# Attention with a pooled branch and a wave MLP: q and k loaded as nine tokens a partition, turned whole and pooled on VectorE

## The chip, the core and the metric

The kernel runs on one core of a Trainium2 chip. A core has a matrix engine (TensorE, PE in the profile, with its weight loads as PEld), a vector engine (DVE), a scalar engine (ACT), a general engine (GpSimd, POOL) and a queue that issues DMAs (SyncE, SP). Operands lie in SBUF, memory of 128 partitions; matrix results go to PSUM, eight banks of 2 KB a partition. The metric is the device time in microseconds of one execution, as the median over runs.

## The reference, cut to what matters

```python
batch, n_heads, seq, head_dim = (8, 8, 576, 64)
# attention, per batch and head
q_d, k_d, v_d = (t.reshape(B, H, 144, 4, D).mean(axis=3) for t in (q, k, v))
out_up = np.repeat(softmax(scale * q_d @ k_d.T) @ v_d, 4, axis=2)
mask = np.abs(pos[:, None] - pos[None, :]) < 4
out_local = softmax(np.where(mask, scale * q @ k.T, -1e9)) @ v
x = (out_up + out_local) as [B, 576, 512]
# wave MLP
theta = x @ w_theta
y = w_tok_r @ (x * cos(theta)) + w_tok_i @ (x * sin(theta))     # over the tokens
u = x + y
out = u + np.maximum(u @ w_ch, 0.0)
```

All inputs and the output are float32; the kernel computes in bfloat16 with float32 sums.

## The kernel before

The eight batches run one after another through the same steps, and the steps of several batches overlap. A string of 682 letters, `ORDER` (lines 85 to 93), says in which order the steps are issued; each letter takes the next step of its kind, through the batches in turn. `pin` (line 691) ties every instruction to the one before it on its engine, so that each engine, and SP's queue too, works through its instructions in the order of the string.

The letters: **L** loads a piece of q, k or v into a staging tile (`load`, line 102; `stage`, line 98; eight tiles of 1024 floats a partition, line 69). **C** casts it to bfloat16 (`cast`, line 131; on GpSimd, but q of batch 0 on ScalarE). **A** turns q and k so that the head's 64 columns lie on the partitions, and makes the pooled q and k; the last A of a batch pools v (`turns`, line 294). **S** makes scores and their exponentials (`scores`, line 376): the first two steps of a batch are the pooled ones, the other five are key chunks of at most 128 keys around a chunk of queries, of which GpSimd blanks all but the band (batch 0 has the band added on TensorE). **N** is the pooled branch's output (three steps), **V** the local one (five), **T** turns and adds the two (five), **H** makes theta, its cosine and sine (five), **Z** the modulated x (four), **X** mixes the tokens (five: four of nine matmuls of 512 columns and a short one), **R** is the channel matmul and **O** the last addition and the store (five each). **z** and **u** are transposing DMAs, **l**, **c** and **W** load, cast and turn the weights, **K** makes constants, **D** keeps TensorE warm.

In batches 0 and 1 (`WIDE`, line 35) q and k are loaded for two heads at once, twelve successive tokens to a partition, 96 partitions: runs of 3072 bytes. In the other batches a token is a partition, 96 to a chunk, and each run is the 64 floats of one head, 256 bytes. v is loaded by key chunks, in runs of 256 bytes, in every batch.

A turn of a token chunk (`turn`, line 325) is four matmuls whose moving operand `ip` is the identity of 96 beside a pooling matrix of 24 columns, so that one pass over 120 columns gives both the turned chunk and its pooled columns; ScalarE evacuates the turned part (line 332), VectorE the pooled q (line 334), ScalarE the pooled k, in up to two pieces (lines 336 to 341), into `kdP`, which has groups of 30 of 32 columns. A wide turn (`wide_turn`, line 303) is eight matmuls with the identity, the last four added up in PSUM for the pooled columns. There are twelve such steps a batch.

PSUM is cut into two tiles of two banks (`w2`, line 78), used in rotation by S, N and V, and four of one bank (`w1`, line 81), used by the others, the turns among them. The key chunks begin at 0, 116, 236, 356 and 448 (`KS`, line 30), each 128 wide.

The weights go through the same staging tiles: theta in two loads, the two token matrices in five each, the channel matrix in two (`weight_loads`, line 235); GpSimd casts them all (line 250).

Of the kernel before, what the change touches and what calls it, by code (L numbers as in the profile page):

```python
# [27 lines left out]
QS = [0, 120, 240, 360, 480]  # L28
QC = [120, 120, 120, 120, 96]
KS = [0, 116, 236, 356, 448]  # L30
KW = [128, 128, 128, 128, 128]
QN = [128, 128, 128, 128, 96]
NCH = 5

WIDE = 2
WR = 12
WP = S // WR
TR = 96
TP = TR // 4
TW = TR + TP  # L40
NG = 3
# [11 lines left out]
def kernel(  # L53
# [15 lines left out]
    stg = ctx.enter_context(tc.tile_pool(name="stg", bufs=8))  # L69
# [11 lines left out]
    def w1(name, dt=FP32):  # L81
# [4 lines left out]
        "LLLKKCCLLLDLLCKACAACALLLCKKCCKKACLLLAKACACALLAALLCASSCCCDDlSSAVAVCSACCAANNAASllcllcNSllLLcTTAlAVVAcC"  # L86
        "HVccllllDAcATTZLLAcccLLccHHSTDWWZCCWLCLSWSWWWWACLZLCSHlVWNNHzLCAALCCCLLSNZAATVAAAATASSXVAAXlCCCSCAVL"
        "LLLLXSVASCccCCTTSTCAASHNXHZVAHHANAuXAHLAACCSSLzLLCZZCCLLuLCRNROROOAVAVAARLLTZSSOXTTSSXVLAAACCCCVXAAT"
        "SSRTHHOVVXANAAAuXCAANAHZHVLLHzLLLLANSSRRRCOuOLOZCRCOZSSZLCTXLLLLACCCSSTTXAAHVVXAARCOATACCCVAANHTZHNA"
        "ZHVZHSzXNVAAXATSSCLLLCCLTZCASHXVZSXAAAVSAAXuAAALCCSSLLTTROLLLTHCCCVRNOHHNHCAXuzNAVAROASSZZLLuXROASVZ"  # L90
        "TTLLRCSSCCCXSOXVTAXAATSSRAAOHNVCLLLuACZCCXNAAXVANAVuROTHVHTRRROOuOVAAVHTHRSSOZRROzOTSROASSROZZHHNNXS"
        "SZTTXHVXHVNHXZXzZZVTXVTTuuXRVHHOTROROZTRRHHOOHXZXXZZzRuuXXOXXRRuOOROXRuRROORROROOO"
# [5 lines left out]
    def stage(b, key):  # L98
        t = staged[b, key] = stg.tile([P, 1024], FP32, tag="st", name=f"st{b}_{key}")
        return t  # L100

    def load(b):

        if b < WIDE:
            for hh in range(4):
                for nm, src in zip("qk", (q, k)):
                    nc.sync.dma_start(
                        out=stage(b, f"{nm}{hh}")[0:TR, 0:WR * D],
                        in_=src[b, 2 * hh:2 * hh + 2].rearrange("h (p r) d -> (h p) (r d)", r=WR),
                    )  # L110
                    yield
        else:
            for nm, src in zip("qk", (q, k)):
                for i in range(3):
                    t = stage(b, f"{nm}{i}")[0:TR].rearrange("p (c h d) -> p c h d", c=2, d=D)
                    for j in range(2):
                        c = 2 * i + j
                        nc.sync.dma_start(
                            out=t[:, j], in_=src[b, :, TR * c:TR * c + TR, :].rearrange("h p d -> p h d"),
                        )  # L120
                    yield
        for i in range(3):
            t = stage(b, f"v{i}").rearrange("p (c h d) -> p c h d", c=2, d=D)
            for c in range(2 * i, min(2 * i + 2, NCH)):
                nc.sync.dma_start(
                    out=t[0:KW[c], c % 2],
                    in_=v[b, :, KS[c]:KS[c] + KW[c], :].rearrange("h p d -> p h d"),
                )
            yield

    def cast(b):

        dims = [TR, 2, WR, 2, D] if b < WIDE else [TR, 6, H, D]
        q_tm = work.tile(dims, BF16, tag="q_tm", bufs=1, name=f"q_tm{b}")
        k_tm = work.tile(dims, BF16, tag="k_tm", bufs=1, name=f"k_tm{b}")
        v_w = v_ws[b % 2]
        inputs[b] = (q_tm, k_tm, v_w)
        eng = CASTS.get(b, CASTS[None])
        if b < WIDE:
            for hh in range(4):  # L140
                for i, dst in enumerate((q_tm, k_tm)):
                    eng[i](out=dst[:, hh // 2, :, hh % 2, :],
                           in_=staged.pop((b, f"{'qk'[i]}{hh}"))[0:TR, 0:WR * D].rearrange("p (r d) -> p r d", d=D))
                    yield
        else:
            for i, dst in enumerate((q_tm, k_tm)):
                for c in range(3):
                    eng[i](out=dst[0:TR, 2 * c:2 * c + 2].rearrange("p c h d -> p (c h d)"),  # L148
                           in_=staged.pop((b, f"{'qk'[i]}{c}"))[0:TR])
                    yield  # L150
        for i in range(3):
            t = staged.pop((b, f"v{i}")).rearrange("p (c h d) -> p c h d", c=2, d=D)
            n, rows = (2, P) if i < 2 else (1, KW[4])
            eng[2](out=v_w[0:rows, 2 * i:2 * i + n, :, 0:D], in_=t[0:rows, 0:n])  # L154
            yield
# [16 lines left out]

    ip = ones("ip", TW, 0.25)
    PU = [ones(f"pu{lo}", KP, 0.25) for lo in (0, 4, 32)]
    own = ones("own", 4, 1.0)
    bands = [ones(f"band{i}", P, 0.0) for i in range(3)]

    def constants():

        pool = ip[0:TR, TR:TW]  # L180
        select(pool, 0, [[-4, TP]], 1)
        select(pool, 3, [[4, TP]], -1)
        nc.vector.tensor_copy(out=ip[0:TR, 0:TR], in_=ident[0:TR, 0:TR])
        yield
# [12 lines left out]


    pihc = const.tile([P, 1], FP32, name="pihc")
    nc.vector.memset(pihc, PIH)  # L200


    kdPs = []
# [542 lines left out]
```

## Time and profile before

| what | value |
|---|---|
| median of 3 runs | 265.8 us (265.38 to 266.84) |
| profiled execution, its own time | 264.21 us |
| its span, from first to last instruction | 262.4 us |
| DMA, mean over the span | 190 GB/s, 49.81 MB, 132483 packets, of which 122592 under 512 bytes |
| mean granted TensorE clock | 0.97 |

The page of the profile gives the busy time of each engine, groups of like instructions with the line that issues them, and a chain of waits: followed back from the last instruction, at each step to what released it. In a group, the first number behind the bar is the busy time of all its instructions in us, the second the mean duration of one in ns, and behind the second bar stands how long the engine had been idle just before them, and who ended that. A busy PE is not PE at its peak, since matmuls overlap one another; the pace of a matmul is read from the chain, which gives start, length, line and count.

### The profile page before, as it was taken

How to read it: one execution, taken by the hardware profiler on the slowest of the kernel's cores; microseconds unless marked ns; L12 is line 12 of the kernel's file. 1: busy time of each engine (PE TensorE's matmuls, PEld its weight loads, DVE VectorE, ACT ScalarE, POOL GpSimd, SP SyncE). 2: the span in 40 equal slices, each digit the busy share in tenths (PEclk: the TensorE clock that was granted, in tenths of full speed). 3: DMA queues.
4: the chain of work that ended last, by engine and by line, in shares of the span. 5: the costliest groups of instructions: out<-in, count | busy, mean ns of one | idle time of the engine just before them, and what ended most of it. 6: DMA issues, size and time to landing. Idle time of an engine off the chain costs nothing.

```text
span 262.4 us, 7363 instructions
## 1 busy us (share of the span) xinstructions
PE 240.0 (91%) x2902; PEld 150.8 (57%) x2938; DVE 171.0 (65%) x391; ACT 169.1 (64%) x338; POOL 162.9 (62%) x196
## 2 busy tenths in 40 slices
PE   3689989969999999999999999999999999999990
PEld 1554755645557655855666566656755556555450
DVE  3331786773666867686885767857978658754552
ACT  3654587895599858986899978849569870340000
POOL 4556946989799879877597599794953750000000
PEclk9858999997999999999999999999999999999998
DMA  7999999999999999999997999999987108145186
GB/s 196 241 236 245 338 228 232 197 228 189 244 194 206 196 169 268 180 216 197 268 203 154 211 180 240 155 222 206 233 222 211 28 0 108 46 141 110 42 216 196
DMA packets 132483, 49.81 MB, mean 190 GB/s; under 512 B 122592, under 2 KB 124640, under 8 KB 132448
## 3 DMA queue, kind: packets, MB, share of 16 engines
q1 hardware_dynamic: 132448, 49.33, 92.8%
q8 instruction: 23, 0.38, 0.6%
q14 instruction: 12, 0.10, 0.1%
HBM read 34.11 MB, written 9.44 MB: 166 GB/s over the span
## 4 chain that ended last, share of the span: by engine, by line
PE 72%; DMA 12%; ACT 6%; POOL 4%; DVE 2%; issue 2%; SPq 1%; DVEq 0%; POOLq 0%; ACTq 0%
PE psu L616 22%; PE psr L646 9%; PE psth L559 8%; PE pstr L329 5%; DMA st_q<-in_q_dram 5%; PE psS L431 4%; PE psloc L503 3%; PE xTps L539 3%; DMA st_k<-in_k_dram 3%; PE psxt L598 3%; DMA out_dram<-osb 3%; PE psut L622 2%; DMA stw_tok<-in_moe_w_tok_i_dram 2%; PE wu L284 2%; PE pstr L308 2%
## 5 line engine op out<-in xcount | busy, mean ns | idle before, releaser
L616 PE MATMUL psu<-WT,z 128*128 128x512 bf16 x276 | 66.6, 381 | 0.9 <-issue 0.4
L439 ACT ACTIVATE pm<-psS 128x1024 bf16<-128x1024 f32 (+1 forms) x40 | 38.1, 991 | 8.5 <-PE psS L431 8.4
L616 PEld LDWEIGHTS <-z 128*128 128x128 bf16 x288 | 26.7, 98 | 29.1 <-issue 0.8
L446 POOL TENSOR_SCALAR_AFFINE_SELECT pm<-pm 128x1024 bf16<-128x1024 bf16 (+1 forms) x35 | 36.8, 1052 | 10.1 <-ACT pm L439 10.1
L617 DVE TENSOR_TENSOR uT<-psu,xT 128x512 bf16<-128x512 f32 x32 | 22.1, 690 | 28.6 <-PE psu L616 28.6
L448 POOL TENSOR_SCALAR_AFFINE_SELECT pm<-pm 128x1024 bf16<-128x1024 bf16 (+1 forms) x35 | 36.8, 1053 | 2.4
L564 ACT ACTIVATE cs<-psth,pihc 128x512 bf16<-128x512 f32 x32 | 22.0, 689 | 16.4 <-PE psth L559 10.5
L559 PE MATMUL psth<-wth,xT 128*128 128x512 bf16 x115 | 31.1, 380 | 0.7
L646 PE MATMUL psr<-wch,uT 128*128 128x512 bf16 x118 | 30.4, 380 | 0.5
L512 DVE TENSOR_TENSOR tmp<-psloc,rl 120x512 bf16<-120x512 f32 (+1 forms) x40 | 27.6, 691 | 1.4
L542 DVE TENSOR_TENSOR xT<-xTps,xdT 128x480 bf16<-128x480 bf16 (+2 forms) x48 | 24.9, 549 | 3.7 <-PE xTps L539 3.3
L668 DVE SCALAR_TENSOR_TENSOR osb<-psr,ur 128x512 f32<-128x512 f32 x32 | 21.6, 685 | 6.4 <-DMA out_dram<-osb 3.8
L154 POOL CAST v_w<-st_v 128x1024 bf16<-128x1024 f32 (+1 forms) x24 | 21.1, 896 | 6.2 <-DMA st_v<-in_v_dram 5.2
L148 POOL CAST k_tm<-st_k 96x1024 bf16<-96x1024 f32 x18 | 18.5, 1035 | 9.3 <-DMA st_k<-in_k_dram 9.3
L332 ACT CAST kT<-pstr 128x384 bf16<-128x384 f32 x36 | 17.8, 497 | 8.2 <-PE pstr L329 8.1
L148 POOL CAST q_tm<-st_q 96x1024 bf16<-96x1024 f32 x18 | 18.6, 1034 | 6.7 <-DMA st_q<-in_q_dram 5.4
L599 DVE TENSOR_TENSOR z<-psxt,cs 128x1024 bf16<-128x1024 bf16 x32 | 21.3, 681 | 1.7 <-PE psxt L598 1.2
L332 ACT CAST qT<-pstr 128x384 bf16<-128x384 f32 x36 | 16.0, 490 | 8.2 <-PE pstr L329 8.1
L565 ACT ACTIVATE cs<-psth 128x512 bf16<-128x512 f32 x32 | 19.0, 594 | 0.0
L503 PEld LDWEIGHTS <-pm 128*128 128x128 bf16 (+1 forms) x320 | 14.9, 103 | 5.6 <-DVE tmp L512 0.8
L503 PE MATMUL psloc<-v_w,pm 128*128 128x65 bf16 (+1 forms) x320 | 17.3, 197 | 0.6 <-DVE tmp L512 0.3
L646 PEld LDWEIGHTS <-uT 128*128 128x128 bf16 x128 | 11.4, 97 | 11.2 <-issue 0.2
(96 smaller groups left out, 427.4 us busy)
## 6 DMA issues: line engine op xcount, KB each, us to landing
st_v<-in_v_dram SPq DMA_DIRECT2D x40, 256.0 KB, 5.3
out_dram<-osb SPq DMA_DIRECT2D x32, 256.0 KB, 2.7
st_q<-in_q_dram SPq DMA_DIRECT2D x36, 192.0 KB, 4.8
st_k<-in_k_dram SPq DMA_DIRECT2D x36, 192.0 KB, 5.0
st_q<-in_q_dram SPq DMA_DIRECT2D x8, 288.0 KB, 6.7
st_k<-in_k_dram SPq DMA_DIRECT2D x8, 288.0 KB, 7.0
stw_tok<-in_moe_w_tok_r_dram SPq DMA_DIRECT2D x4, 288.0 KB, 8.0
stw_tok<-in_moe_w_tok_i_dram SPq DMA_DIRECT2D x4, 288.0 KB, 5.6
```

Of the source, the lines that this page charges most:

```text
L148: eng[i](out=dst[0:TR, 2 * c:2 * c + 2].rearrange("p c h d -> p (c h d)"), in_=staged.pop((b, f"{'qk'[i]}{c}"))[0:TR])
L332: nc.scalar.copy(out=To[:, :, TR * c:TR * c + TR], in_=ps[:, :, 0:TR])
L439: nc.scalar.activation(out=pv, in_=ps[0:kw].rearrange("p e (j w) -> p (e j) w", w=P)[:, :, 0:qn], func=AF.Exp, scale=SCL,)
L446: nc.gpsimd.affine_select(out=pv, in_=pv, compare_op=ALU.is_ge, fill=0.0, base=off, pattern=[[0, 8], [-1, qn]], channel_multiplier=1)
L448: nc.gpsimd.affine_select(out=pv, in_=pv, compare_op=ALU.is_ge, fill=0.0, base=6 - off, pattern=[[0, 8], [1, qn]], channel_multiplier=-1)
L503: nc.tensor.matmul(out=pv[0:qn, h // 4, h % 4, :], lhsT=pms[b][c][0:kw, 4 * par + blk, 0:qn], rhs=v_w[0:kw, c, h, 0:65], start=(h % 4 == 0 ...
L512: nc.vector.tensor_tensor(out=tmp[0:cnt].rearrange("p (e j d) -> p e j d", e=2, j=4), in0=pv[0:cnt, :, :, 0:D], in1=rl[0:cnt].unsqueeze(3) ...
L542: nc.vector.tensor_tensor(out=dst.rearrange("p e (m j) -> p e m j", j=4), in0=ps[:, :, lo:lo + n].rearrange("p e (m j) -> p e m j", j=4), ...
L559: nc.tensor.matmul(out=th, lhsT=xA[:, dc, P * c:P * c + P], rhs=wth[:, dc, :], start=(dc == 0), stop=(dc == 3),)
L616: nc.tensor.matmul(out=ps, lhsT=z[:, j, P * dc:P * dc + P], rhs=WT[:, j, 0:MAIN], start=(j == 0), stop=(j == 8))
L617: nc.vector.tensor_tensor(out=uA[:, dc, :], in0=ps, in1=xA[:, dc, :], op=ALU.add)
L646: nc.tensor.matmul(out=psr, lhsT=uA[:, dc, P * c:P * c + P], rhs=wch[:, dc, :], start=(dc == 0), stop=(dc == 3),)
```

## The change

All batches now load q and k as batches 0 and 1 did, with nine tokens to a partition: 128 partitions of 576 floats (2304 bytes), two heads to a load, eight loads a batch. Each v chunk is a load and a cast of its own, so a batch has thirteen L and thirteen C. There are fifteen staging tiles of 576 floats.

A turn is nine transposes of 128 x 128 into one two-bank tile, taken in rotation with S, N and V; a batch has four of them (q and k of each half of the heads), so five A with the pooling of v. ScalarE evacuates each in two copies of 576 elements. The pooled q and k are then sums over four neighbouring columns, made by VectorE from the turned copies in SBUF. For the last chunk `kT` has 24 columns of zeros behind the 576, in two tiles that are made once.

Key chunks begin at multiples of 120 and query chunks at 0, 124, 244, 364 and 484, so one pooling matrix serves all and two band matrices are left. The pooled branch's turned output is copied by ScalarE. The weights are staged in tiles of the later steps (`ur`, `xT`, `z`), the channel matrix in four loads through the staging tiles; VectorE casts the second token matrix. An exponential is run on a constant at the start. The order of the steps is another string, of 674 letters.

```diff
-QS = [0, 120, 240, 360, 480]
-QC = [120, 120, 120, 120, 96]
-KS = [0, 116, 236, 356, 448]
-KW = [128, 128, 128, 128, 128]
+QS = [0, 124, 244, 364, 484]
+QC = [124, 120, 120, 120, 92]
+KS = [0, 120, 240, 360, 480]
+KW = [128, 128, 128, 128, 96]
...
-WIDE = 2
-WR = 12
+WR = 9
...
-    stg = ctx.enter_context(tc.tile_pool(name="stg", bufs=8))
+    stg = ctx.enter_context(tc.tile_pool(name="stg", bufs=15))
...
+        "LKCLCLLCACLLLLLLKAKCCLLCCCLDKAAlLLLlLCCDCSSSCCLLASSLNNLVVllllCllNcCLLVCcCTALLLLLTASCccCcTSCHVVcDTZCCC"
+        "ATAHlllHlHZZcHSDZLlLLLLWlccCCCcASSccDzlNCCCSWWWSLNWWCCLLLLLLLLLClCSWCCCCCSWWVAXVANXAACXVXSLTTLLLSuAC"
+        "CVSTHTVNHHNLTZZCACCVcLLLLccLcHCCHXzLCZLLSRLLROOZCCCuCLLLLLAARLLLARLSSXCCSCSOOXVVCCCCXSNCVSTAVTCCSROT"
+        "ATATCCLLCSXSSHNuHNVXZZAALLCAVHHVCCHNRRzOSSTOCLLCCLLRORLOLLuSCCTZZTSSCHVXVTAHCCNNLXLLZTANAHHLCCVVLLCH"
+        "XACACSCLLLLXVXCCzLRSLLLSLLLOTLLLTZZCCSCZATALLuLXSLSHHVNXVNZTXTCAACCCCHHCCHVSuXXRSSROOzCZVNTRRCCSSOOR"
...
-            ps = w1(f"pstr{n}{c}_{b}")[:, 0:4 * TW].rearrange("p (hh w) -> p hh w", w=TW)
-            for hh in range(4):
-                nc.tensor.matmul(
-                    out=ps[:, hh, :], lhsT=tm[0:TR, c, 2 * hh:2 * hh + 2, :], rhs=ip[0:TR, :], start=True, stop=True,
-                )
-            nc.scalar.copy(out=To[:, :, TR * c:TR * c + TR], in_=ps[:, :, 0:TR])
...
+            ps = w2(f"pstr{n}{i}_{b}", BF16).rearrange("p k e -> p (k e)")[:, 0:WR * P]
+            for r in range(WR):
+                nc.tensor.transpose(out=ps[:, P * r:P * r + P], in_=tm[:, i, r, :, :], identity=ident)
+            for a in range(2):
+                act(
+                    out=To[:, 2 * i + a, 0:S].rearrange("p (w r) -> p w r", r=WR),
+                    in_=ps.rearrange("p (r a w) -> p a w r", r=WR, a=2)[:, a],
+                )
             hs = slice(2 * i, 2 * i + 2)
...
+            dst, src = (qdT[:, hs, :], qT[:, hs, :]) if n == 0 else (kdP[:, hs, :, 0:30], kT[:, hs, :])
+            src = src.rearrange("p e (m j) -> p e m j", j=4) if n == 0 else src.rearrange("p e (g m j) -> p e g m j", g=5, j=4)
...
+                nc.vector.tensor_reduce(out=dst, in_=src, axis=AX.X, op=ALU.add)
...
-        nc.vector.tensor_copy(out=xds[b], in_=ps)
+        act(out=xds[b], in_=ps)
...
-                gp(out=w_tm[ri][0:OC[ct], ct, :], in_=staged.pop(("w", f"tok{ri}{ct}"))[0:OC[ct], 0:S])
+                src = staged["w", ri][:, ct, :] if ct < 4 else staged["w", "tail"][0:OC[4], ri, :]
+                (gp, dve)[ri](out=w_tm[ri][0:OC[ct], ct, :], in_=src)
```

194 lines of the change are left out of this document (68 added, 126 removed).

## The prediction

> **What bounds the kernel now.** I read the page first, then busy time by stretch, then the chain of waits, then the groups by engine.
>
> ```profile
> span 262.4 us, 7363 instructions
> ## 1 busy us (share of the span) xinstructions
> PE 240.0 (91%) x2902; PEld 150.8 (57%) x2938; DVE 171.0 (65%) x391; ACT 169.1 (64%) x338; POOL 162.9 (62%) x196
> ```
>
> TensorE is busy for 91% of the span, the next engine for 65%. A busy PE need not be a fast one, so I ask where its idle time lies. Columns of the stretches: PE, PEld, DVE, ACT, POOL, then the granted clock, the DMA share and GB/s.
>
> ```profile
> 0.00:43.00 43.00, 33.51 (x402) 21.26 (x406) 21.36 (x80) 23.79 (x56) 25.16 (x51) 0.88 1.06 250
> 43.00:61.00 18.00, 15.26 (x230) 10.90 (x229) 12.63 (x30) 15.82 (x31) 16.43 (x18) 0.94 1.11 198
> ```
>
> ```profile
> 60.00:180.00 120.00, 117.53 (x1505) 75.44 (x1523) 83.47 (x176) 96.77 (x195) 100.32 (x106) 0.99 1.12 207
> ```
>
> From 60 to 180 us PE is busy 117.5 of 120 us: there only PE work, or a new wait, can move the time. Before that it idles 9.5 us in 43 and 2.7 us in 18. The chain of waits says what the opening waits for:
>
> ```profile
> 37.40 5.59 DMA stw_tok<-in_moe_w_tok_i_dram
> 43.05 0.67 POOL wtm L257
> ...
> 61.09 0.54 PE psu L616
> ```
>
> The last token-mixing weight lands at 43.0 us, and the first mix (the first X of the order) starts at 61.1. From then on PE has always something to do, so I split the change there: when does the first mix start, how much PE work is behind it, and which new wait stands in that work?
>
> **The start.** The weight that lands last (the twelfth l) stands behind other loads on SP's queue. Before, these are 16 loads of q, k (96 x 768 floats, 288 KB), 7 of v (256 KB), 1024 KB of theta and 2592 KB of the token weights: 10.0 thousand KB, 10.3 MB. They were through at 43.0 us; less the 0.8 us before the first issue that is 243 GB/s, and the window 0 to 43 shows 250. After, 27 L stand in front: 17 of q, k (128 x 576 floats, again 288 KB), 10 of v (2432 KB), and the same weights: 10.9 thousand KB, 11.2 MB. At 243 GB/s that takes 46.1 us, so the weight lands at 46.9, some 4 us later. The fifteen staging tiles take all of batch 0 and two loads more without a wait for a cast, and theta and the token weights have tiles of their own, so I price no wait of the SP queue here. Other end: the rate is that of larger packets.
>
> ```profile
> 24.00:32.00 8.00, 7.10 (x130) 4.91 (x122) 5.76 (x15) 4.66 (x15) 7.02 (x10) 1.00 1.06 326
> ```
>
> In these 8 us, in which token weights (rows of 2304 bytes, as q, k get now) came in, the core moved 326 GB/s. If all 5.0 MB of q, k go at that rather than at 250 GB/s, they take 15.4 us in place of 20.0, and the weight lands at about 42.
>
> What stands between that landing and the first mix? In the old order 62 letters: four H, seven S, nine W, ten A, three each of N, T and Z, two V, one D. In the new one: eight W, four S, two N, and one each of D, V and A. For their PE time I take paces from the chain (an entry is start, length, line, count):
>
> ```profile
> 98.90 0.42 PE pstr L329 x8
> 99.32 0.21 PE xTps L539 x4
> 99.53 0.55 PE psS L431 x16
> ...
> 102.65 0.51 PE psloc L503 x16
> 103.16 1.94 PE psu L616 x9
> ...
> 106.45 1.05 PE psut L622 x36
> ```
>
> Per step: an X 1.94 (its last 1.05); a matmul of 512 columns 0.216, so an H or R of four 0.86; an S 0.28; a V 0.26; a T 0.21, a Z little more; an old turn (four matmuls of 120 columns) 0.21, or 0.052 a matmul. A new turn is nine transposes of 128 columns: 9 x 0.052 x 128/120 = 0.50. A W (five transposes) is 0.28, an N about 0.5, a D 1.3 (six of 512). The old 62 letters come to 14 us of PE, the new ones to 6.4. PE was busy 15.3 of 18.0 us there, 85%, so 6.4 / 0.85 = 7.5 us. First mix at 46.9 + 7.5 = 54.4; I take 55, **-6.1 us**. Ends: 50 (the faster rate, -11), and 61 or later (0), if the steps ahead of that landing aren't done by 47 us.
>
> **PE work behind the first mix.** The same 40 X, 40 R and 35 H remain. Of turns, the old order has 63 left (13.2 us), the new one 23 (11.6 us): -1.6. But the new one has done less else: one V, one N and two T more remain (0.26 + 0.26 + 0.42). Net **-0.7 us**. The cheaper turns of batches 0 and 1 lie ahead of the first mix and are inside the first term. The tail (15 X after the last turn, ten R and O of the last two batches) is the same work in another order; nothing for it, give or take 2.
>
> **VectorE.** Its groups (duration is the second number behind the bar):
>
> ```profile
> L512 DVE TENSOR_TENSOR tmp<-psloc,rl 120x512 bf16<-120x512 f32 x32 | 22.1, 692 | 1.1
> L617 DVE TENSOR_TENSOR uT<-psu,xT 128x512 bf16<-128x512 f32 x32 | 22.1, 690 | 28.6 <-PE psu L616 28.6
> L668 DVE SCALAR_TENSOR_TENSOR osb<-psr,ur 128x512 f32<-128x512 f32 x32 | 21.6, 685 | 6.4 <-DMA out_dram<-osb 3.8 <-PE psr L646 2.0 <-DMA ur<-uT 0.5
> L599 DVE TENSOR_TENSOR z<-psxt,cs 128x1024 bf16<-128x1024 bf16 x32 | 21.3, 681 | 1.7 <-PE psxt L598 1.2 <-ACT cs L565 0.5
> L542 DVE TENSOR_TENSOR xT<-xTps,xdT 128x480 bf16<-128x480 bf16 x32 | 20.1, 650 | 2.6 <-PE xTps L539 2.3
> L478 DVE TENSOR_TENSOR xd<-psnd,rd 72x512 bf16<-72x512 f32 x16 | 11.0, 687 | 0.5
> L334 DVE CAST qdT<-pstr 128x96 bf16<-128x96 f32 x36 | 9.0, 254 | 8.1 <-ACT qT L332 6.4
> L510 DVE RECIPROCAL rl<-psloc 120x8 f32<-120x8 f32 x32 | 6.4, 200 | 12.0 <-PE psloc L503 11.9
> L313 DVE CAST kT<-pstr 128x384 bf16<-128x384 f32 x12 | 6.3, 549 | 0.6 <-PE pstr L308 0.5
> L579 DVE TENSOR_TENSOR zT<-xT,cst 128x512 bf16<-128x512 bf16 x8 | 5.8, 729 | 5.8 <-ACT cst L577 5.7
> ...
> L276 DVE COPY WT<-wps 128x576 bf16<-128x576 bf16 x9 | 4.1, 455 | 1.7 <-PE wps L271 1.7
> L319 DVE CAST qdT<-pstr 128x96 bf16<-128x96 f32 x12 | 3.8, 320 | 9.4 <-ACT qT L313 9.2
> L491 DVE COPY xdT<-psxd 128x576 bf16<-128x576 bf16 x8 | 3.6, 447 | 0.1
> L624 DVE TENSOR_TENSOR uT<-psut,xT 128x256 bf16<-128x256 f32 x8 | 3.4, 423 | 1.6 <-PE psut L622 1.5
> ```
>
> The trace has no reduction. It reads 1152 elements (q: 2 x 144 x 4) or 1200 (k: 2 x 5 x 30 x 4). From L624 to L617 an element costs (690 - 423) / 256 = 1.04 ns, so 690 + 640 x 1.04 = 1.36 us for q and 1.41 for k, 1.38 on average, which I take: it is the row of most groups here. Low end: two elements a cycle, as in L599 (0.51 ns an element past 157 ns fixed): 0.74. High end: L579, bf16 from the same memory, 1.42 ns an element with all fixed cost in it: 1.64 for q. The Trainium skill ("VectorE: DVE Perf Modes", section "The perf-mode tier table (the rule you actually need)") speaks against this change: it gives tensor_reduce one element a cycle whatever the type, with only a 1x program. No trace here shows it; by it the low end falls away and the forecast stays, while 0.74 would take the 1.6 us of the next paragraph but one off it.
>
> Thirty-two reductions are 44 us. Away go 36 x 0.254 + 12 x 0.320 (qdT), 12 x 0.549 (kT), 8 x 0.447 (xdT, to ScalarE) = 23.1; five casts of 576 elements come, at most 549 + 192 x 1.04 = 0.75 each, least L276's 0.455, in the opening where DVE was busy 21 of 43 us: nothing. Per batch from 2 on: +5.5 - 1.5 - 0.4 = +3.6. DVE was busy 83.5 of 120 us (60 to 180); 27 of the 36 L334 casts, so four and a half batches, lie there: +16, or 83%.
>
> An average hides the tight places, so I count the 153 letters from the second V of batch 1 to the third of batch 3. DVE: 11 reductions 15.2, 12 V at 0.892 10.7, 4 N 3.5, 10 T 6.6, 6 Z 4.1, 9 X 5.7, 5 O 3.2, one H 0.7: 49.7 us. PE: 9 X 15.7, 9 H 7.4, 5 R 3.9, 11 turns 5.5, 14 S 3.9, 12 V 3.1, 6 N 2.6, 10 T 2.1, 6 Z 1.4, 3 last A 0.9: 46.5. There DVE has 3.2 us more than PE. Behind a 1.38 us reduction stand the adds and multiplies that empty PSUM (X, V, Z, T), for which PE's next steps wait; the pooled scores (S) wait for the reduction itself. Since neighbouring stretches have room, I take half, **+1.6 us**; ends 0 and 9.4 (3.2 and 0.27 more for each of the 23 reductions behind the first mix).
>
> **ScalarE, GpSimd and PSUM.** A turn's two evacuations read 576 elements each.
>
> ```profile
> L332 ACT CAST kT<-pstr 128x384 bf16<-128x384 f32 x36 | 17.8, 497 | 8.2 <-PE pstr L329 8.1
> L332 ACT CAST qT<-pstr 128x384 bf16<-128x384 f32 x36 | 16.0, 490 | 8.2 <-PE pstr L329 8.1
> ...
> L414 ACT ACTIVATE pd<-psSd 128x576 bf16<-128x576 f32 x8 | 5.3, 660 | 2.3 <-PE psSd L408 2.3
> L358 ACT CAST vd<-psva 128x512 bf16<-128x512 f32 x8 | 4.7, 588 | 4.0 <-PE psvb L356 4.0
> ```
>
> A cast of 512 takes 588 ns and an activation of 576 takes 660, so about 0.64 us. Per batch 12 x 0.49 = 5.9 us and the pooled columns' copies become 8 x 0.64 = 5.1 and one xdT of 0.64: no more than before. GpSimd has half of the token weights' casts less and about as many bytes of q, k, v. On SP's queue a batch's q, k are eight issues in place of twelve, so the stores and turning DMAs between them wait for less. All counted nothing: PE hides them, and none gets longer.
>
> But a turn now takes one of the two large PSUM tiles, which S, N and V use too: 18 fills a batch in place of 14. In the 153 letters there are 41 fills in 46.5 us; with two tiles each may be held 2.27 us. A turn holds one for 0.50 + 1.28 = 1.8, an S some 1.3, a V or N 1.2: 60% on average, against 39% of a longer cycle without the turns. Where A, A or A, S, S follow one another, PE waits. I take **+0.5 us**; ends 0 and 4 (a third of 23 turns waiting for half an exponential).
>
> **Sum.** -6.1 - 0.7 + 1.6 + 0.5 = -4.7 us. The profiled execution took 264.21 us (1.8 outside its span), so 259.5; the median of the runs shown is 265.8, 1.6 more, so the same difference gives **261.1 us**.
>
> **Rivals.** (1) The opening gains more and DVE costs nothing: q, k at 326 GB/s, first mix at 50, -11 - 0.7 = -11.7: 254.1. For it: packets of 2304 bytes for every q, k. Against it: v keeps 256-byte runs, and the core already moved 250 GB/s. (2) The opening gains little: the weight lands 4 us later and the work ahead of it, done partly at a granted clock of 0.88, isn't finished: first mix at 59.5, -1.6 - 0.7 + 2.1 = -0.2: 265.6. (3) VectorE becomes the bound, slower: reductions at 1.64 us and queues behind them, +9.4, with PSUM's +4: -6.1 - 0.7 + 13.4 = +6.6: 272.4. It decides between the first mix and the last turns. With PSUM's 0.5, DVE must give back 6.3 us; 3.2 are there if no neighbour has room, and 3.1 over 23 reductions are 0.13 more each: from about 1.5 us a reduction it is slower. For it: 49.7 against 46.5. Against it: 70% busy now.
>
> **How the numbers follow.** What a measurement can tell from no change is about 0.5%, 264.5 to 267.1 us. Forecast 0.42 (own range 257 to 264.4), rival 1 0.18, rival 2 0.14, rival 3 0.26. Faster 0.60, same 0.14, slower 0.26. The range, 252.5 to 271, reaches rival 1's time with a margin and most of rival 3's.
>
> **What would show it.** The first psu in the chain of waits at 55 us, with stw_tok landing at 47; a reduction's duration at 1.4 us; DVE at 83 to 86% from 60 to 180 us with PE still over 95%. Waits of PE for DVE in the middle, or psS, psloc and pstr waiting for ScalarE, are rivals. A reduction of 1.6 us or a first mix at 60 us proves me wrong.

## The result, and the profile after

The kernel with the change takes 253.68 us (median of four runs, 253.15 to 253.86), the kernel before 265.59 in the four runs that stand for it here (264.4 to 266.84): a ratio of 0.955, with a 95% interval of 0.950 to 0.960. The forecast of 261.1 us had the direction right and the range held the time, but the gain is 11.9 us where 4.7 were forecast. Between the two profiled executions it is 264.21 - 253.52 = 10.7. Of the kernels told of below, one (256-byte runs for all batches) was over 1.5% slower than its fastest execution in three of ten; its time is the median of the other seven.

The head of the page of the kernel after:

```profile
span 251.8 us, 6875 instructions
## 1 busy us (share of the span) xinstructions
PE 230.9 (92%) x2746; PEld 141.3 (56%) x2746; DVE 192.8 (77%) x357; ACT 159.0 (63%) x245; POOL 152.1 (60%) x211
```

VectorE has 21.8 us more work than before, and TensorE is still the fullest engine. Where the time went is read with the mark that the prediction used, the first mix. The view of one tile, `psu`, gives of each operation its shortest, median and longest duration in ns, and the first and last start in us; before, then after:

```profile
L616 PE MATMUL psu<-WT,z x276: 377/379/610, 61.0 to 246.9; 128*128 128x512 bf16 x138
```

```profile
L564 PE MATMUL psu<-WT,z x288: 377/379/390, 51.5 to 237.3; 128*128 128x512 bf16 x144
```

The first mix starts at 51.5 us instead of 61.0 (9.5 us; 9.6 with the chain's 61.09). From the first to the last of these matmuls it is 185.9 us before and 185.8 after. From the first mix to the end of the span it is 201.4 before and 200.3 after. So nearly the whole gain lies in the opening, and behind it some 1 us, in the tail. The same stretches as before, of the kernel after (PE, PEld, DVE, ACT, POOL, granted clock, DMA share, GB/s):

```profile
0.00:43.00 43.00, 30.37 (x337) 17.71 (x339) 24.87 (x66) 29.08 (x46) 23.15 (x46) 0.96 0.99 277
43.00:61.00 18.00, 17.85 (x213) 11.40 (x213) 15.76 (x28) 10.95 (x17) 17.07 (x22) 1.00 1.14 286
60.00:180.00 120.00, 116.97 (x1532) 75.19 (x1531) 105.24 (x179) 91.93 (x142) 97.37 (x130) 1.00 0.86 203
```

The core moves 277 and 286 GB/s in the first 61 us where it moved 250 and 198. From 60 to 180 us VectorE is busy 88% of the time instead of 70%, and PE 0.6 of 120 us less. The pooled sums and the turns' copies cost what was worked out for them (groups of the page):

```profile
L295 DVE TENSOR_REDUCE qdT<-qT 128x288 bf16<-128x1152 bf16 x16 | 21.6, 1350 | 11.6 <-ACT qT L287 11.5
...
L287 ACT COPY qT<-pstr 128x576 bf16<-128x576 bf16 x32 | 19.0, 647 | 9.7 <-PE pstr L285 9.6
...
L295 DVE TENSOR_REDUCE kdP<-kT 128x300 bf16<-128x1200 bf16 x16 | 22.3, 1396 | 1.7 <-ACT kT L287 1.7
```

The chain of waits of the kernel after, up to the first mix (start, length, what; x is a count):

```profile
1.72 4.81 DMA st_q<-in_q_dram
...
12.70 1.19 ACT qT L287 x2
13.91 1.35 DVE qdT L295
15.27 1.32 DVE kdP L295
...
21.82 0.61 POOL k_tm L122
...
26.22 0.62 POOL k_tm L122
...
40.74 1.28 ACT L345
42.03 0.62 ACT pd L345
42.82 0.58 ACT vd L306
43.65 1.63 POOL vd L310 x2
...
45.32 0.27 PE psnd L419
...
51.17 0.50 PE pstr L285 x9
51.67 0.43 PE psu L564 x2
```

In the kernel before, this chain went through three transfers: the fourth q load, a k load and the token weight that the prediction shows; the first two of them are:

```profile
3.60 7.55 DMA st_q<-in_q_dram
...
29.32 7.18 DMA st_k<-in_k_dram
```

Now only one transfer is left, at the start. What follows are copies on ScalarE, two reductions on VectorE, GpSimd's casts one behind the other (20.6 to 26.8), exponentials and sines, and (40.74) an entry of 1.28 us that names no tile, ahead of an exponential. The timeline names it:

```profile
40.74 1.28 ACT L345 ACT_TABLE_LOAD   x1
```

Entries of this name and length stand where ScalarE changes between exponential and sine. Behind the one at 0.80 us there are four of them ahead of the first mix in the kernel before (two are in its chain, at 50.41 and 54.29) and two in the kernel after, so ScalarE has 2.6 us less of them there; what that is worth wasn't tried. From 45.3 us on the chain is PE's own work, the turns of the token weights (`wps`) among it. The landing of the last token weight isn't in it, though that landing (43.4 us) and the first mix (51.5) are 8.1 us apart, close to the 7.5 that the prediction had put there. Whether that is a coincidence was one of the questions for the experiments.

### The profile page after: what moved, and what is told of

It is laid out like the page before. It is cut to its first block, busy times and chain, and to the rows that moved or that the text cites. A ratio compares the mean times of both kernels' runs of the same rounds, so it can differ in the third digit from the quotient of the medians.

```text
span 251.8 us, 6875 instructions
## 1 busy us (share of the span) xinstructions
PE 230.9 (92%) x2746; PEld 141.3 (56%) x2746; DVE 192.8 (77%) x357; ACT 159.0 (63%) x245; POOL 152.1 (60%) x211
## 4 chain that ended last, share of the span: by engine, by line
PE 77%; ACT 9%; DMA 4%; POOL 3%; DVE 3%; issue 2%; SPq 1%; DVEq 0%; ACTq 0%; POOLq 0%
PE psu L564 25%; PE psth L507 10%; PE psr L594 7%; PE pstr L285 6%; PE psloc L451 4%; PE psS L379 4%; PE psut L570 3%; PE xTps L487 3%; ACT qT L287 3%; PE psxt L546 3%; DMA out_dram<-osb 2%; DMA st_q<-in_q_dram 2%; ACT kT L287 2%; DVE osb L616 2%; PE psnd L413 2%
## 5 line engine op out<-in xcount | busy, mean ns | idle before, releaser
L295 DVE TENSOR_REDUCE qdT<-qT 128x288 bf16<-128x1152 bf16 x16 | 21.6, 1350 | 11.6 <-ACT qT L287 11.5
L122 POOL CAST k_tm<-st_k 128x576 bf16<-128x576 f32 x32 | 21.5, 670 | 13.5 <-DMA st_k<-in_k_dram 12.3
L460 DVE TENSOR_TENSOR tmp<-psloc,rl 120x512 bf16<-120x512 f32 (+2 forms) x40 | 27.6, 690 | 1.4
L490 DVE TENSOR_TENSOR xT<-xTps,xdT 128x480 bf16<-128x480 bf16 (+3 forms) x48 | 25.2, 547 | 3.6 <-PE xTps L487 3.6
L126 POOL CAST v_w<-st_v 128x512 bf16<-128x512 f32 (+1 forms) x40 | 23.3, 612 | 4.8 <-DMA st_v<-in_v_dram 4.8
L287 ACT COPY qT<-pstr 128x576 bf16<-128x576 bf16 x32 | 19.0, 647 | 9.7 <-PE pstr L285 9.6
L295 DVE TENSOR_REDUCE kdP<-kT 128x300 bf16<-128x1200 bf16 x16 | 22.3, 1396 | 1.7 <-ACT kT L287 1.7
L287 ACT COPY kT<-pstr 128x576 bf16<-128x576 bf16 x32 | 19.1, 658 | 6.3 <-PE pstr L285 6.3
L122 POOL CAST q_tm<-st_q 128x576 bf16<-128x576 f32 x28 | 18.8, 671 | 3.1 <-DMA st_q<-in_q_dram 2.2
L513 ACT ACTIVATE cs<-psth 128x512 bf16<-128x512 f32 x32 | 19.7, 616 | 0.0
```

The lines of the kernel that those rows point to most:

```text
L122: eng[i](out=dst[:, hh // 2, :, hh % 2, :], in_=staged.pop((b, f"{'qk'[i]}{hh}")).rearrange("p (r d) -> p r d", d=D))
L287: act(out=To[:, 2 * i + a, 0:S].rearrange("p (w r) -> p w r", r=WR), in_=ps.rearrange("p (r a w) -> p a w r", r=WR, a=2)[:, a],)
L295: nc.vector.tensor_reduce(out=dst, in_=src, axis=AX.X, op=ALU.add)
L460: nc.vector.tensor_tensor(out=tmp[0:cnt].rearrange("p (e j d) -> p e j d", e=2, j=4), in0=pv[0:cnt, :, :, 0:D], in1=rl[0:cnt].unsqueeze(3) ...
L490: nc.vector.tensor_tensor(out=dst.rearrange("p e (m j) -> p e m j", j=4), in0=ps[:, :, lo:lo + n].rearrange("p e (m j) -> p e m j", j=4), ...
```

## The experiments

Two questions were open. Where do the 9.6 us of the opening come from: the form of the loads, the cheaper turns, the staging, the order, the time at which the weight lands? And why did VectorE's 22 us more cost nothing, and how far is it from costing something? All times below are medians; "behind" is the span less the start of the first mix, and "clock" the mean granted TensorE clock up to the first mix, these three of the profiled execution. Each ratio is to executions of the kernel before from the same set, whose median lies between 264.58 and 265.59 us, so times of different sets can be 1 us apart without a cause in the kernels. A kernel built from the one before is told as "old", from the one after as "new".

| run | us | ratio to before, 95% interval | first mix | behind | clock |
|---|---|---|---|---|---|
| before | 265.59 | 1 | 61.0 | 201.4 | 0.90 |
| after | 253.68 | 0.955 [0.950, 0.960] | 51.5 | 200.3 | 0.97 |
| new, 256-byte runs for q, k of batches 0 and 1 | 259.57 | 0.976 [0.970, 0.982] | 58.5 | 200.2 | 0.94 |
| new, the same for batch 0 alone | 254.89 | 0.962 [0.958, 0.965] | 53.0 | 200.3 | 0.97 |
| new, the same for batch 1 alone | 255.46 | 0.965 [0.960, 0.969] | 52.6 | 200.2 | 0.97 |
| new, the same for all batches | 268.0 | 1.011 [1.007, 1.015] | 58.4 | 208.4 | 0.97 |
| old, loads of 128 partitions x 2304 bytes | 261.28 | 0.985 [0.981, 0.989] | 58.8 | 200.9 | 0.95 |
| old, long runs in batches 2 to 7 | 264.26 | 0.997 [0.994, 1.001] | 61.0 | 202.0 | 0.95 |
| old, weights in tiles of their own | 264.96 | 0.998 [0.995, 1.001] | 61.2 | 201.7 | 0.99 |
| new, token weights issued earlier | 253.5 | 0.956 [0.950, 0.962] | 50.8 | 200.4 | 0.97 |
| new, 0.44 us more a reduction | 257.34 | 0.969 [0.963, 0.975] | 53.5 | 202.7 | 0.94 |
| new, every reduction twice | 282.24 | 1.063 [1.052, 1.074] | 57.8 | 221.2 | 0.94 |
| new, a short copy for the reduction | 252.7 | 0.953 [0.948, 0.958] | 49.4 | 200.8 | 1.00 |
| new, no warm-up matmuls | 256.09 | 0.965 [0.960, 0.970] | 54.3 | 200.4 | 0.94 |
| new, k copied by VectorE in batches 0, 1 | 260.25 | 0.981 [0.975, 0.987] | 58.8 | 200.4 | 0.91 |
| the same, token weights earlier | 260.39 | 0.982 [0.978, 0.986] | 58.8 | 200.3 | 0.91 |

The last column matters for small differences. In the old kernel the clock of the opening costs nothing that can be seen: at 0.90 and at 0.99 (weights in tiles of their own) the first mix starts at 61.0 and 61.2 us, and executions of the kernel before with a mean clock of 0.991 and 0.968 took 264.75 and 264.77. In the new kernels lower clocks and longer times go together: of the four executions with k copied by VectorE, the one with a mean clock of 0.989 took 257.67 us, those with 0.975 to 0.982 took 260.02 to 261.01. An estimate from the column: at 0.97 the opening of the kernel after loses 0.03 x 51.5 = 1.5 us of PE's clock, at 0.94 about 3.2, at 0.91 about 5.3. So among the new kernels a shift of the first mix by some 2 us isn't told apart from the clock.

**The form of the loads, taken back.** In the new kernel only the q, k loads of batches 0 and 1 are cut into runs of 256 bytes (rows of 66 floats in the staging tile, so that the runs can't be joined); everything else, the order too, stays.

```diff
-        t = staged[b, key] = stg.tile([P, S], FP32, tag="st", name=f"st{b}_{key}")
+        t = staged[b, key] = stg.tile([P, WR * 66], FP32, tag="st", name=f"st{b}_{key}")
...
-                    out=stage(b, f"{nm}{hh}"),
-                    in_=src[b, 2 * hh:2 * hh + 2].rearrange("h (p r) d -> (h p) (r d)", r=WR),
+                        out=t.rearrange("p (r d) -> p r d", d=66)[:, :, 0:D],
+                        in_=src[b, 2 * hh:2 * hh + 2].rearrange("h (p r) d -> (h p) r d", r=WR),
```

> The kernel after, with q and k of batches 0 and 1 landing in runs of 256 bytes. Theory L (the opening got shorter because loads land faster): 16 loads go from 0.75 to some 1.4 us, 10 us more of DMA time ahead of the last token weight; the first mix moves from 51.5 to 57 to 62 us, the time from 253.7 to 259 to 264. Theory O (the new order alone did it, by what it puts behind the last weight): first mix within 2 us of 51.5, time within 2 us of 253.7.

The first mix moved from 51.5 to 58.5 us and the time by 5.9 us, half of the gain (at a clock of 0.94 instead of 0.97, so up to 2 us of it may be the clock's). Its stretch from 0 to 43 us:

```profile
0.00:43.00 43.00, 25.82 (x263) 15.02 (x266) 19.87 (x57) 23.34 (x35) 20.24 (x41) 0.94 1.08 224
```

The core moves 224 GB/s at a DMA share of 1.08 where it moved 277 at 0.99: the same engines, as full, with fewer bytes. In the transfers of the trace the first eight loads land every 1.3 us in this kernel, every 0.75 to 0.8 from the third on in the kernel after, and every 1.2 us in the kernel before, with its 96 partitions of 3072 bytes.

**And for all batches.** The same edit without the condition on the batch.

> The same for all batches. Theory L with the loads hidden behind the first mix: no more than 2 us above the run with batches 0 and 1 alone; DMA share from 60 to 180 us up from 0.86 to 1.1, PE still busy 97% there. Rival S (faster loads also took waits out of the middle): 4 us or more above it.

```profile
60.00:180.00 120.00, 109.33 (x1401) 69.58 (x1418) 96.28 (x163) 85.32 (x132) 96.45 (x129) 1.00 1.05 217
```

```profile
PE 34%; DMA 29%; POOL 21%; SPq 8%; issue 4%; DVE 2%; ACT 1%; POOLq 0%; DVEq 0%
```

Another 8.4 us, nearly all of it behind the first mix (208.4 instead of 200.2), and the kernel is 1.1% slower than the one before. PE is busy for 109.3 of the 120 us, and the chain of waits (the second fence: its shares by engine) runs through DMA and GpSimd for half of the span; GpSimd's casts of k wait 23.4 us for their loads. So the new kernel lives on the fast loads throughout: it is not only the opening that would suffer without them.

**Does the old kernel suffer there?** It loads q, k of batches 2 to 7 in runs of 256 bytes. Here it loads them in runs of 2048 (the values are then not the right ones, the amounts are).

```diff
-                            out=t[:, j], in_=src[b, :, TR * c:TR * c + TR, :].rearrange("h p d -> p h d"),
+                            out=t[:, j].rearrange("p h d -> p (h d)"),
+                            in_=src[b].rearrange("h s d -> (h s d)")[TR * DM * c:TR * DM * c + TR * DM].rearrange("(p e) -> p e", e=DM),
```

> The kernel before with q and k of batches 2 to 7 loaded in runs of 2048 bytes from consecutive addresses, the same bytes in as many loads; the values so stand in the wrong places, so the attention of these batches is not the reference's. Theory L (short runs cost time in the kernel before too): 3 to 6 us faster than before, 259.5 to 262.5. Theory O (the old order hid them): within 1.5 us of before.

```profile
60.00:180.00 120.00, 119.63 (x1524) 75.74 (x1522) 83.12 (x176) 96.46 (x195) 101.82 (x108) 0.98 0.91 209
```

The DMA share falls from 1.12 to 0.91 and PE is busy 119.6 of 120 us, but the time stays within what can be told from no change. The old order had hidden the short runs behind PE's work; a cheaper transfer that nobody waits for gains nothing.

**The fast loads in the old order.** Batches 0 and 1 of the old kernel with loads of 128 partitions x 2304 bytes, the same bytes; the cast then takes six of a partition's nine tokens twice, so that it, and all behind it, costs as before.

```diff
-                        out=stage(b, f"{nm}{hh}")[0:TR, 0:WR * D],
-                        in_=src[b, 2 * hh:2 * hh + 2].rearrange("h (p r) d -> (h p) (r d)", r=WR),
+                        out=stage(b, f"{nm}{hh}")[:, 0:S],
+                        in_=src[b, 2 * hh:2 * hh + 2].rearrange("h (p r) d -> (h p) (r d)", r=9),
```

> The kernel before with the 16 wide loads of batches 0 and 1 as 128 partitions x 2304 bytes in place of 96 x 3072, the same bytes; the casts read as many elements as before but the wrong ones, so the attention of these two batches is not the reference's. Theory L (the rate of these loads sets the opening): a load 0.75 us in place of 1.2, first mix 55 to 58 us in place of 61.1, time 3 to 6 us less. Theory O (what the old order puts ahead of the first mix sets it): first mix at 60 or later, time within 1.5 us of before.

```profile
L617 PE MATMUL psu<-WT,z x276: 377/379/631, 58.8 to 244.0; 128*128 128x512 bf16 x138
```

The last token weight lands at 38.3 us instead of 43.8, and the first mix starts 2.2 us earlier, not 5.5. That lies between the two theories; the time, 3.9 us below the kernel before of the same set (265.18), is as theory L had it. With the run before, four cases of the first mix stand side by side:

```
                             old kernel   new kernel
slow loads (1.2 to 1.3 us)      61.0         58.5
fast loads (0.75 us)            58.8         51.5
```

The loads alone bring 2.2 us, the rest of the change alone 2.5, and both together 9.5: about half of the gain exists only with both. With slow loads the new kernel waits for them; with fast loads the old one doesn't use them fully, for what stands in its opening behind them. (The two kinds of slow load aren't the same, 1.2 and 1.3 us, and the clocks differ, so the split is good to some 2 us.)

**Batch 0 or batch 1?** The condition of the first experiment, on one batch each.

> The kernel after with q and k of batch 0 alone in runs of 256 bytes. Theory Q (everything queues behind these loads, so any 4.6 us of slower loads ahead of the weight shift the opening alike): first mix 3 to 4 us later than 51.5, as with batch 1 alone. Theory F (only the first loads are waited for, the rest is engine work): 4 to 7 us later here and under 1.5 us with batch 1 alone.

> The same for batch 1 alone. Theory Q: first mix 3 to 4 us later. Theory F: under 1.5 us later.

First mix at 53.0 and 52.6, so +1.5 and +1.1, where both together are +7.0. Neither theory foretold that pair: batch 1 alone fits F, batch 0 alone neither. Neither batch alone is the one that matters: the opening bears one batch's slower loads with little loss, and not those of two. The clock was 0.97 with one batch and 0.94 with both, so part of the difference may be the clock's.

**Staging.** The weights of the old kernel in tiles of their own, as the change has it, so that they don't wait for staging tiles.

```diff
-        yield from two(moe_w_theta, "th")
+        for i in range(2):
+            wst = staged["w", f"th{i}"] = moep.tile([P, 1024], FP32, tag="ur", name=f"th{i}")
...
+            wst = staged["w", ri] = moep.tile([P, 4, S], FP32, tag="z", name=f"tok{ri}")
```

> The kernel before, with theta and the token weights staged in the later steps' tiles as in the kernel after, nothing else changed. Theory L: the loads go no faster, first mix 59 to 61 us, time within 2 us of before. Rival G (the staging tiles held the loads up): first mix at 56 us or earlier, 4 us or more faster than before.

No difference that can be told: first mix at 61.2. In the old order, where the weights are staged brings nothing.

**The landing of the weight.** The prediction's start term was the landing of the last token weight and 7.5 us of work. Here the order of the new kernel has the last four l letters 37 letters and more earlier (`NcCLLVC` becomes `NcCLllllLVC`, `ATAHlllHlHZZ` becomes `ATAHHHZZ`).

> The kernel after with the last four loads of the second token matrix issued ahead of batch 1's five v loads, so that the last weight lands at about 38 us in place of 43.4 and batch 1's v some 3 us later. If that landing alone sets the first mix: 46 to 48 us, time 249 to 251. If the chain of waits is right, which comes to the first mix through ScalarE's exponentials and sines and GpSimd's vd from 35 to 45 us and not through the weight: first mix within 1 us of 51.5, time within 1 us of 253.7.

The view of the weight's last piece (tile `tail`), of this run:

```profile
L220 SPq DMA_DIRECT2D tail<-in_moe_w_tok_i_dram x1: 504/504/504, 28.2 to 28.2; - x1
...
L234 DVE CAST wtm<-tail x1: 859/859/859, 44.0 to 44.0; 64x576 bf16<-64x576 f32 x1
...
DMA to landing us min/median/max: 6.6/7.4/8.1
```

It is issued at 28.2 and lands 6.6 us later, at 34.8 us, 8.6 earlier than in the kernel after (36.3 + 7.1 = 43.4). The first mix moves by 0.7 us, and the time not at all. VectorE comes to the cast of that piece at 44.0 us here and at 44.7 in the kernel after, in the order of its own work, so an earlier landing is of no use to it. The landing isn't what the first mix waits for: the chain of waits said so, and the 8.1 us between the two was a coincidence.

**Reductions: how much more would VectorE bear?** In the first kernel a second, short reduction of 288 elements stands behind each one; in the second kernel one of 1152, written to a tile that nothing reads.

Written out for the short one (a cut):

```diff
+    extra = const.tile([P, 288], BF16, name="extra")
...
+                more = To[:, 2 * i, 0:288].rearrange("p (m j) -> p m j", j=4)
+                nc.vector.tensor_reduce(out=extra[:, 0:72], in_=more, axis=AX.X, op=ALU.add)
```

> The kernel after with a second reduction of 288 elements (some 0.46 us) behind each of the 32, into a tile that nobody reads: 14.7 us more on VectorE, 10.5 of them behind the first mix. Theory N (the stretches next to the tight ones have room): at most 2.5 us more, 253.7 to 256. Theory B (VectorE is as tight as TensorE): 8 to 12 us more, 262 to 266. By the prediction a reduction of over 1.5 us makes the kernel slower than before (265.6); this is 1.84 in sum.

> The same with the whole reduction made twice: 44 us more on VectorE, which would be 237 of 252 us, and over 120 in the 120 us from 60 to 180. Theory N: VectorE becomes the bound in the middle only, 10 to 20 us more (264 to 274). Theory B: 32 us or more (over 285).

The added groups and the stretch from 60 to 180 us, first of the small one, then of the full one:

```profile
L298 DVE TENSOR_REDUCE extra<-qT 128x72 bf16<-128x288 bf16 x16 | 7.1, 442 | 0.0
```

```profile
60.00:180.00 120.00, 116.37 (x1481) 73.26 (x1479) 109.85 (x194) 90.17 (x140) 99.75 (x133) 1.00 0.85 198
```

```profile
L298 DVE TENSOR_REDUCE extra<-qT 128x288 bf16<-128x1152 bf16 x16 | 21.5, 1342 | 0.0
```

```profile
60.00:180.00 120.00, 105.62 (x1318) 65.43 (x1315) 112.71 (x170) 82.26 (x127) 86.94 (x118) 0.97 0.78 186
```

14.2 us more work on VectorE (32 x 0.442) cost 3.7 us in the medians; in the profiled executions 2.0 ahead of the first mix, where the clock was lower too (0.94 instead of 0.97), and 2.4 behind it. 43 us more cost 28.6, of which 21 behind the first mix, with VectorE busy for 94% of the time and PE for 88% from 60 to 180 us. So VectorE becomes the bound, but beyond the reductions of 1.37 us: with the small one, 1.8 us a turn, the kernel is still 8.2 us faster than before. The two durations also give the price of an element: (1342 - 442) / 864 = 1.04 ns. It is the price that the prediction took from the additions with a float32 operand. The Trainium skill ("VectorE: DVE Perf Modes", section "The perf-mode tier table (the rule you actually need)") gives tensor_reduce only a 1x program, and these rows agree.

**And if it cost less?** The reduction becomes a copy of every fourth column, on average 583 and 517 ns instead of 1350 and 1396 (so q and k aren't pooled but sampled).

```diff
-                nc.vector.tensor_reduce(out=dst, in_=src, axis=AX.X, op=ALU.add)
+                nc.vector.tensor_copy(out=dst, in_=src[:, :, :, 0] if n == 0 else src[:, :, :, :, 0])
```

> The kernel after with each reduction replaced by a copy of every fourth column (288 or 300 elements, some 0.4 us for 1.38): the pooled q and k are not sums, so the pooled branch is not the reference's. About 31 us less on VectorE. If the reductions are covered: 0 to 2.5 us less than 253.7. If they cost what the small extra did, 0.23 us for each us on VectorE: about 7 us less, 246 to 248.

First mix at 49.4, 2.1 us earlier; behind it 200.8 instead of 200.3. The reductions cost nothing behind the first mix, and in the opening at most about 2 us: the clock there was 1.00 instead of 0.97, which alone can bring 1.5. In the total the intervals of the two kernels overlap.

**Warm-up matmuls.** The five D of the order (30 matmuls whose results nothing reads) left out.

> The kernel after without the 30 warm-up matmuls. If they only take time, 3.9 us of them being in the chain of waits of the opening: first mix at 48 to 49 us, time 250 to 252. If they keep the granted clock up: the clock falls below 0.9 in the first 40 us, the first mix stays at 51 us or comes later, time 254 or more.

```profile
0.00:43.00 43.00, 26.57 (x309) 16.56 (x312) 24.56 (x65) 28.23 (x44) 23.12 (x46) 1.00 1.01 286
43.00:61.00 18.00, 16.09 (x185) 10.92 (x187) 12.70 (x26) 10.78 (x18) 16.00 (x21) 0.81 1.08 278
```

2.4 us slower, with the first mix at 54.3. The work was less (PE 26.6 us from 0 to 43 instead of 30.4), but the granted clock in the 18 us behind is 0.81 instead of 1.00. The fall below 0.9 in the first 40 us that was expected did not come: there the clock is 1.00, and 0.96 with the D letters. The low clock has moved: with them it is 0.79 from 16 to 24 us, where PE is busy for 6.3 of 8 us, without them 0.57 from 44 to 52, where it is busy for 7.2. The D letters, one of which the prediction had counted as work ahead of the first mix, pay for themselves.

**ScalarE's copies in the opening.** In the chain of the kernel after ScalarE has the most entries. So the copies of k in batches 0 and 1 (eight of 0.65 us) go to VectorE, in the order of the kernel after and in that with the earlier weights.

```diff
-                act(
+                (dve if n == 1 and b < 2 else act)(
```

> The kernel after with the turned k of batches 0 and 1 evacuated by VectorE in place of ScalarE: eight copies of 0.65 us less in ScalarE's part of the chain, four of them from batch 1, two of which the chain of waits shows (35.8 to 36.9 us). If the chain through ScalarE sets the first mix: 1 to 3 us earlier, time 251 to 252.7. If the loads set it: within 0.5 us of 51.5.

> Both edits, k by VectorE in batches 0 and 1 and the last weight's loads early. If ScalarE's chain sets the first mix and the weight is next behind it: 1.5 to 4 us earlier than 51.5, time 249.5 to 252.5, below both kernels. If the loads set it: as the kernel after, within 1 us.

The chain of waits of the first:

```profile
42.15 1.35 DVE qdT L295
43.51 0.51 DVE xT L490 x2
44.02 1.34 DVE kT L287 x2
45.38 1.41 DVE kdP L295
...
49.80 3.59 DVE wtm L234 x5
```

The gain that was looked for turned into a loss: they are 6.6 and 6.7 us slower than the kernel after, with the first mix at 58.8 in both. The copies that left ScalarE now stand on VectorE between the two reductions, one behind the other: 4.1 us a turn pair where it was 2.7. Behind them VectorE comes late to the casts of the second token matrix, which end at 53.4 us where they ended at 45.6. So VectorE, though only 58% busy up to 43 us in the kernel after, has no room there for these copies. A part of the loss is the clock's, 0.91 instead of 0.97 up to the first mix: at a mean clock of 0.989 an execution took 257.67 us with these copies and 253.86 without. Whether ScalarE's copies set the first mix of the kernel after is not shown by this.

**The loads by themselves.** A kernel without the computation, which loads only, eight loads of each form one behind another. The first one filled the eight tiles anew ahead of each form, and the loads waited for these fills: their issues were about 1.07 us apart, whatever the form, so it told nothing of the rate.

> Leaves out the whole computation: eight loads each of six shapes, one shape after the other, then zeros to the output. What is read is the time from one landing to the next. Both theories: 128 partitions x 2304 bytes 0.75 us and 96 x 3072 bytes 1.2 us, as in the two kernels. Theory P (the number of partitions decides): 96 x 2304 about 0.9 us, 128 x 3072 about 1.0. Theory R (the length of the run decides): 96 x 2304 0.56 us, 128 x 3072 1.6. Runs of 256 bytes on 128 partitions (288 KB) 1.2 to 1.6 us by both.

The second one, without the fills between the forms, so that the loads queue:

> As m_loads, leaving out the whole computation, without the fills between the shapes, which set the pace there. By theory P (partitions decide): 128 x 2304 0.75 us from landing to landing, 96 x 3072 1.2, 96 x 2304 0.9, 128 x 3072 1.0. By theory R (the run's length decides): 0.75, 1.2, 0.56, 1.6.

Stretches in which the packets of one form alone were under way, in this order: 128 partitions x 2304 bytes; 96 x 3072; 96 x 2304; 128 x 3072; 128 x nine runs of 256; 96 x eight runs of 256 (columns: us, DVE, POOL, clock, DMA share, GB/s):

```profile
19.00:21.00 2.00, 0.31 (x2) 0.00 (x0) 1.00 1.02 383
24.00:30.00 6.00, 0.93 (x6) 0.00 (x0) 1.00 1.03 263
32.00:36.00 4.00, 0.61 (x4) 0.00 (x0) 1.00 1.06 271
39.00:45.00 6.00, 0.92 (x6) 0.00 (x0) 1.00 1.04 399
49.00:57.00 8.00, 1.08 (x7) 0.00 (x0) 1.00 1.16 224
58.00:63.00 5.00, 0.92 (x6) 0.00 (x0) 1.00 1.36 206
```

At the same length of run, 96 partitions move 263 and 271 GB/s, 128 partitions 399 and 383: 0.66 and 0.71 of it, somewhat less than the three quarters that the partitions are. From landing to landing it is 1.11, 0.82 and 0.98 us for the second to the fourth form: theory P. The length of the run (2304 or 3072) hardly matters. With runs of 256 bytes both are slow, and the partitions hardly matter (206 and 224). The kernel before had the two slow forms for q and k, the kernel after has the fast one.

## Why the prediction was right or wrong, point by point

**The first mix, -6.1 us: the step that failed.** Of the 6.0 us by which the gain between the profiled executions (10.7) exceeds the 4.7 forecast, 3.5 lie here and 2.5 in the terms behind the first mix. The prediction put the first mix at 46.9 + 7.5 us, the landing of the last weight and the work behind it. Two things in it were off. The rate: "at 243 GB/s that takes 46.1 us" took the old mean for the new loads. The kernel after lands that weight at 43.4, which is nearer to the other end named there, 42. What the text held against a better rate were v's short runs, which stay; the loads by themselves show that the old q, k loads were slow too, for their 96 partitions. The other thing is the wait itself: with the weight 8.6 us earlier the first mix moved by 0.7, so "landing + 7.5" is not what starts it. What does, by the chain of waits, is a path through ScalarE, VectorE, GpSimd and PE, fed by the loads of batches 0 and 1: it comes to PE at 45.3 us with GpSimd's `vd`, and from there to the mix PE works without a break for 6.3 us, where 6.4 of PE work were counted. So the size of the work was about right, and it hung on the wrong event. Measured: -9.6 instead of -6.1. (The 43.0 us that the prediction gives the twelfth piece of the kernel before is the landing of the eleventh; the twelfth lands at 43.8.)

**PE work behind the first mix, -0.7 us.** Together with the next two terms, +1.4 us was forecast behind the first mix; measured were -1.1. PE's busy time from 60 to 180 us fell from 117.5 to 117.0, and the tail behind the last mix got about 1 us shorter, which the text had left at "give or take 2". A new turn takes the 0.50 us that was worked out (51.17 in the chain). Whether the -0.7 as a whole is right can't be read: 12 of the 288 records of `psu` are missing in the trace of the kernel before.

**VectorE, +1.6 us.** The duration was right: 1.36 and 1.41 us worked out from other operations' rows, 1.35 and 1.40 measured. So was the busy share, nearly: 88% against 83 to 86. But it cost nothing that can be seen behind the first mix (the short copy in its place brings nothing there), and at most about 2 us ahead of it, where the text had counted nothing. "From about 1.5 us a reduction it is slower" fell: with 1.8 us a turn the kernel is 8.2 us faster than before. The count of letters had taken a stretch as a bound of its own and half of its 3.2 us as lost; what was lost is nothing that can be seen, so the neighbouring stretches gave back all of it.

**PSUM, +0.5 us.** Nothing of it shows, but it wasn't tried by itself.

**Costed at nothing.** ScalarE's copies (0.65 us, 0.64 worked out) are right, but in the opening they are in the chain of waits. The staging: in the old order it makes no difference (61.2 us). The SP queue in the middle: "PE hides them" holds only because the loads are long; with runs of 256 bytes the new kernel loses 8.2 us there.

**The rivals.** The first (254.1 us: more gain in the opening, VectorE free) came nearly true, for another reason than its own: not the rate alone, which brings 2.2 us in the old order. The second, a late weight and an unfinished opening, did not come. The third, VectorE as the bound, exists, but needs reductions well over 1.8 us; with them doubled the kernel takes 282 us.

**What stays open.** Of the opening's 9.6 us, 2.2 are the loads alone and 2.5 the rest alone; how these 2.5 and the other half divide among the order, the cheaper turns, the two ACT_TABLE_LOAD fewer and ScalarE's shorter list was not taken apart. Nor was tried what an earlier `vd` would bring.

## What to carry to other kernels

The start of a kernel is a chain through several engines; the last transfer to land is a candidate for its end, not its cause, until the chain of waits names it, and issuing it earlier is a cheap way to ask. Before a rate of before is used for loads of another form, look at how many partitions and how long a run each load has: here the form of the loads and the rest of the change brought half of the gain only together, and the same transfers made faster where nobody waited for them brought nothing. An engine at 88% can be free where its neighbours have room, and on the path where it is at 58%: ask it stretch by stretch, and by adding a little work. Before two openings are compared to 2 us, look at the granted clock of each.

## What the runs showed of the hardware that had not been expected

- A load into 96 partitions moves 271 and 263 GB/s, into 128 partitions 383 and 399, with runs of 2304 and of 3072 bytes. The DMA share is 1.06 and 1.03 in the first case and 1.02 and 1.04 in the second, so the profile shows no idle engines that would explain it. An estimate from share and rate: a packet of 2304 bytes keeps one of the 16 engines busy for 144 ns with 96 partitions (1.06 x 16 x 2304 / 271) and for 98 with 128. The Trainium skill ("DMA: Bandwidth & Descriptors", section "The descriptor swizzle") says of a transfer to 128 partitions issued from GpSimd that eight of the sixteen engines serve partitions 0 to 63, and eight those from 64 on. If that held for these loads too, 96 partitions would take as long as 128 of the same row, three quarters of the rate, with half of the engines idle for a part of it; measured are 0.71 and 0.66 of the rate at shares that are no lower, so these rows don't bear it out, and the cause stays open.
- Runs of 256 bytes move 224 GB/s into 128 partitions where runs of 2304 move 383, and 206 into 96.
- Thirty matmuls without a use shorten the kernel by 2.4 us: without them the granted clock is 0.81 from 43 to 61 us, with them 1.00, though up to 43 us it is 1.00 without them and 0.96 with them.
